# Six casts of value-weight sums behind the first tile's exponentials, and four raw row stores issued by SyncE

## The chip, the cores and the metric

The kernel runs on one core of one Trainium2 chip. The metric is the device time of one execution, in microseconds (us); smaller is better. Before the change it is 1594.4 us, the median of three runs (1594.2 to 1595.8).

## What is computed

A layer norm without weights feeds two branches, and their results are joined on the input. Sequence length S = 2048, width D = 576, 32 heads of 18 columns, hidden width F = 4608, all in float32.

```python
xn = _layernorm(x)
# branch A: linear attention with learned features
q, k, v = split_heads(xn @ wqkv)                  # 32 heads of 18
pq, pk = q @ w_phi, k @ w_phi                     # one 18x18 matrix per head
phi_q = concat(softmax(pq), softmax(-pq))
phi_k = concat(softmax(pk), softmax(-pk))
kv = sum over s of phi_k[s] (outer) v[s];  z = sum over s of phi_k[s]
s  = (phi_q @ kv / (phi_q @ z + 1e-6)) @ wo
# branch B: gated feed-forward
g  = silu((silu(xn @ w_gate) * (xn @ w_up)) @ w_down)
out = x + s * g
```

## The kernel before

Every float32 operand of a matmul is split into a rounded high part (a cast on ScalarE, ACT in the profile) and a low part (the operand minus the high part, on VectorE = DVE or GpSimd = POOL), and a product takes three matmuls: high by high, high by low, low by high. TensorE is PE in the profile, SyncE is SP. Names such as TH and TL are the high and the low part of one matrix.

The work has four stages. The **first** (0 to 61 us of the trace) reads x in four blocks of 512 rows, normalizes them, turns them with PE, splits them into `XB`, folds `w_phi` into the q and k weights, and computes the first tiles of the feed-forward as filler for PE. The order of all this is written out by hand: the wrappers `PE`, `ACT`, `DVE`, `POOL` and `SP` of class `InOrder` keep each engine's instructions in the order of the program text. Blocks are taken in the order b = 2, 3, 0, 1. For each block `x_raw(b)` (line 271) copies 64 turned columns from PSUM to a tile `xr` on ScalarE and stores it into `x_dram` with two DMAs, which ScalarE issues. `xr` has one buffer; GpSimd reads it too (`x_rest_low`, line 266) for blocks 3, 0 and 1.

The **second** stage (61 to about 221 us) computes k, its features, v, and the sum kv over 16 row tiles of 128. `k_tile` (line 653) makes the product for k in PSUM (`p`), then `softmax_parts` (line 525): DVE takes maxima and minima per head and subtracts them (lines 530 and 531), ScalarE takes the exponentials (line 534, two per tile, collected in `exps`), DVE sums (538), takes reciprocals (661) and scales (662) to `phi`. `v_plain` (line 671) makes half of v in one of the PSUM banks vx, vy, vw, and `v_copy` (646) copies it on ScalarE into `vbuf`. `kv_step` (line 543) adds phi times v to `kvp` on PE, one tile later than phi was begun.

From the fifth tile on, v is computed with Strassen's scheme, which needs sums and differences of blocks of x ("stacked sums", `raw_x`, `sums`, `sum_parts`, lines 560 to 582) and of the value weights (`v_sums(c)`, line 589, for the three row chunks c = 0, 1, 2). `v_sums(c)` loads two rows of weights with SyncE (line 599), makes four sums on GpSimd (600 to 603), and then twice casts a sum on ScalarE into TH (606) and takes the low part on GpSimd (608 for c < 2, 610 for c = 2). The buffers of c = 0 (`sraw`) are used again by c = 2 and afterwards by the stacked sums; those of c = 1 by other loads (line 121 among them). All three calls stand in the program after the first tile's `k_tile` and `v_plain`, and before the second tile's. `v_first` (612) needs PE to be done with a part of the value weights.

The **third** stage (to 491 us) makes q, the attention output and more feed-forward tiles, the **fourth** the rest of the feed-forward.

Outside the first stage the compiler's scheduler orders each engine's queue: it takes instructions by priority (earlier in the program first, `tc.high_priority()` ahead) as they become ready in its own estimate of time. An engine executes its queue strictly in that order. `tc.issue_after(ins)` adds an edge: the block's instructions on the engine of `ins` are queued behind `ins`. It adds no semaphore.

Of the kernel before, what the change touches and what calls it, by code (L numbers as in the profile page):

```python
# [61 lines left out]
def gated_hedgehog_kernel(ctx: ExitStack, tc, x, w_qk, w_v, consts_in, wo, w_gu, w_tail, w_down, out):  # L62
# [5 lines left out]
    nc = tc.nc  # L68
# [19 lines left out]
    x_dram = dram.tile([2, 4, P, 4, P], F32, name="x_dram")  # L88
# [67 lines left out]
    with ExitStack() as att:  # L156
# [18 lines left out]
        with ExitStack() as wst:  # L175
# [4 lines left out]
            with ExitStack() as pst:  # L180
# [12 lines left out]
                PE, ACT, DVE, POOL, SP = (InOrder(tc, e) for e in (nc.tensor, nc.scalar, nc.vector, nc.gpsimd, nc.sync))  # L193
# [77 lines left out]
                def x_raw(b, ps):  # L271
                    xr = prep.tile([P, 2, BT], F32, name="xr", bufs=1)
                    ACT.copy(xr, ps)
                    for m in range(2):
                        ACT.dma_start(x_dram[b // 2, :, :, b % 2 * 2 + m].rearrange("s p n -> p s n"),
                                      xr[:, m].rearrange("p (s n) -> p s n", s=4))
                    return xr

                def fold(m, g, ps=None):
# [90 lines left out]
                t = slice(8, 12)  # L370
# [22 lines left out]
                ACT.copy(first_weights[0][1][0], raws[1])  # L393
                part_low(first_weights[0][1], raws[1])
                x_raw(2, ps)
                load_x(1)
                half(0, 0)
# [10 lines left out]
                for n in range(6):  # L408
                    o = n * D if n < 3 else 832 + (n - 3) * D
                    wv[n] = ahead[1 if n < 3 else 3][:, o:o + D]  # L410
                    k, c = V_PLACES[n]
                    SP.dma_start(wv[n], w_v[:, k, c])
                stat(12, 13, 14, 15)
                t = slice(12, 16)
# [25 lines left out]
                for c in range(2):  # L440
                    x_high(3, c, tops[c])
                    x_low(3, c, tops[c])
                x_rest_high(3, tops[2])
                xr = x_raw(3, tops[2])
                x_rest_low(3, POOL, xr)
                stat(2, 3)
# [8 lines left out]
                t = slice(0, 8)  # L455
# [26 lines left out]
                for c in range(2):  # L482
                    x_high(0, c, tops[c])
                    x_low(0, c, tops[c])
                x_rest_high(0, tops[2])
                xr = x_raw(0, tops[2])
                x_rest_low(0, POOL, xr)
                products(1, 1, 1, "h0 h1")
# [18 lines left out]
                xr = x_raw(1, tops[2])  # L507
# [8 lines left out]
            TH = kt.tile([P, 3, 3, HALF], F32R, name="TH")  # L516
# [24 lines left out]
            kk_pool, read, exps = kk, [], []  # L541
# [47 lines left out]
            def v_sums(c):  # L589
                if c == 1:  # L590
                    u = epool.tile([P, 2, 3, P], F32, name="raw", bufs=2).rearrange("p a b n -> p (a b n)")[:, 0:D]
                    l = kk.tile([P, 4, 2, P], F32, name="slo", bufs=1).rearrange("p a b n -> p (a b n)")[:, 0:D]
                else:
                    t = kk.tile([P, 4, 3, P], F32, name="sraw", bufs=1).rearrange("p a b n -> p (a b n)")
                    u, l = t[:, 0:D], t[:, D:2 * D]
                u, l = (t.rearrange("p (m n) -> p m n", m=2) for t in (u, l))
                add, sub = nc.gpsimd.tensor_add, nc.gpsimd.tensor_sub
                for k, t in enumerate((u, l)):
                    nc.sync.dma_start(t, w_v[:, k, c].rearrange("p (m n) -> p m n", m=2))
                sub(l[:, 0], l[:, 0], u[:, 0])  # L600
                sub(t1[:, c] if c < 2 else t1t, u[:, 0], u[:, 1])
                add(u[:, 1], u[:, 1], l[:, 0])
                sub(l[:, 1], l[:, 1], u[:, 1])
                for m, t in ((0, u[:, 1:2]), (slice(1, 3), l)):
                    m = slice(0, 1) if m == 0 else m
                    nc.scalar.copy(TH[:, m, c], t)
                    if c < 2:
                        nc.gpsimd.tensor_sub(TL[:, m, c], t, TH[:, m, c])
                    else:
                        nc.gpsimd.tensor_sub(TH[64:96, m, 2], t[64:96], TH[64:96, m, 2])  # L610
# [71 lines left out]
            for p in range(8):  # L682
                k = (p + 4) % 8
                ts = [k // 4 * HT + k % 4 + 4 * j for j in range(2)]
                if p < 2:
                    for j, t in enumerate(ts):
                        phi = k_tile(t)
                        v_plain(t, vbuf[j], 0)
                        if pend is not None:
                            if not kvp:  # L690
                                kvp += [kps.tile([GW, 4, GW + 1], F32, name=f"kvp{i}") for i in range(3)]
                            kv_step(*pend)
                        v_plain(t, vbuf[j], 1)
                        pend = (2 * p + j, phi, vbuf[j])
                        if p == 0 and j == 0:
                            for c in range(3):
                                v_sums(c)
                        elif p == 0:
                            load_stack(order[0])
                            raw_x(order[0], 0, 1)  # L700
                            raw_x(order[0], 2, 3)
                        elif j == 0:
                            sums(order[0])
                    if p == 1:
                        v_first()
                        sum_parts(order[0])
                        load_stack(order[1])
                    continue
# [750 lines left out]
```

## Time and profile before

| what | value |
|---|---|
| median of the runs | 1594.4 us (1594.2, 1594.4, 1595.8) |
| the profiled execution's own time | 1593.34 us |
| its span (first to last instruction) | 1591.5 us |
| mean granted clock of PE | 0.998 |
| DVE, ACT, POOL busy | 73%, 46%, 42% |

How to read what follows. A timeline row has the start (us from the span's start), the length, the engine, the line, the operation, output and inputs with shapes, a count, and in brackets the idle time of the engine before it with what ended that. Neighbouring instructions of one kind are merged into one row with a count, and its length then runs from the first start to the last end. Instructions of the first stage that are kept in order by hand all have line 50, the wrapper's. An engine name with a q (SPq, ACTq) is its sequencer, here issuing DMAs. PE and PEld are one engine's matmuls and weight loads. A row of the chain has start, length, engine, tile, line and count.

### The profile page before, as it was taken

How to read it: one execution, taken by the hardware profiler on the slowest of the kernel's cores; microseconds unless marked ns; L12 is line 12 of the kernel's file. 1: busy time of each engine (PE TensorE's matmuls, PEld its weight loads, DVE VectorE, ACT ScalarE, POOL GpSimd, SP SyncE). 2: the span in 40 equal slices, each digit the busy share in tenths (PEclk: the TensorE clock that was granted, in tenths of full speed). 3: DMA queues.
4: the chain of work that ended last, by engine and by line, in shares of the span. 5: the costliest groups of instructions: out<-in, count | busy, mean ns of one | idle time of the engine just before them, and what ended most of it. 6: DMA issues, size and time to landing. Idle time of an engine off the chain costs nothing.

```text
span 1591.5 us, 25302 instructions
## 1 busy us (share of the span) xinstructions
PE 1574.4 (99%) x9371; PEld 1417.9 (89%) x9371; DVE 1166.4 (73%) x1720; ACT 729.3 (46%) x1406; POOL 672.4 (42%) x725
## 2 busy tenths in 40 slices
PE   9899999999999999999999999999999999999998
PEld 7799998999988898898888898888888888888887
DVE  7577769999957778887777778645667667666677
ACT  6633345454535645454444544454343343333334
POOL 5755672444116635644545445223324324133133
PEclk9999999999999999999999999999999999999999
DMA  9414344446448554555555453975545565556445
GB/s 288 144 57 146 113 135 137 123 124 195 138 148 270 178 177 171 180 172 179 175 177 202 159 192 116 338 218 151 154 139 154 183 188 160 175 184 185 142 118 179
DMA packets 123303, 269.05 MB, mean 169 GB/s; under 512 B 12452, under 2 KB 54116, under 8 KB 121900
## 3 DMA queue, kind: packets, MB, share of 16 engines
q1 hardware_dynamic: 108620, 245.67, 47.1%
q0 software_dynamic: 3552, 12.59, 2.8%
q10 hardware_dynamic: 11008, 9.18, 1.8%
q8 instruction: 74, 1.21, 0.3%
q14 instruction: 49, 0.40, 0.1%
HBM read 167.54 MB, written 99.09 MB: 168 GB/s over the span
## 4 chain that ended last, share of the span: by engine, by line
PE 92%; DVE 2%; POOL 2%; ACT 1%; issue 1%; DMA 1%; SPq 0%; ACTq 0%; POOLq 0%
PE px L1006 25%; PE pd L1127 24%; PE pw L1006 12%; PE p L108 7%; PE py L1006 6%; PE pe L108 5%; PE p L888 4%; PE kvp L547 2%; PE pt L860 2%; PE vx L635 1%; PE pt L853 1%; PE vw L635 1%; PE vx L108 0%; PE vy L108 0%; DMA wst<-in_A_w_qk 0%
## 5 line engine op out<-in xcount | busy, mean ns | idle before, releaser
L1127 PEld LDWEIGHTS pd<-dw,hh 128*128 128x128 f32 x3012 | 423.4, 188 | 22.7 <-ACT pd L1182 1.5
L1127 PE MATMUL pd<-dw,hh 128*128 128x288 f32 x3012 | 437.7, 295 | 2.1 <-ACT pd L1182 0.7
L1006 PE MATMUL px<-X,w 128*128 128x512 f32 x1512 | 385.7, 390 | 0.0
L1006 PEld LDWEIGHTS px<-X,w 128*128 128x128 f32 x1512 | 274.6, 188 | 46.0
L1006 PE MATMUL pw<-X,w 128*128 128x512 f32 x744 | 188.8, 389 | 0.0
L1006 PEld LDWEIGHTS pw<-X,w 128*128 128x128 f32 x744 | 139.6, 188 | 28.9
L1289 DVE TENSOR_TENSOR acc<-pd,acc 128x576 f32<-128x576 f32 x128 | 96.3, 753 | 92.6 <-PE pd L1127 92.1
L1040 DVE TENSOR_TENSOR s<-pw,s 128x512 f32<-128x512 f32 x126 | 86.4, 687 | 89.6 <-ACT s L1035 79.2
L1035 ACT COPY s<-px 128x512 f32<-128x512 f32 x126 | 73.8, 586 | 145.4 <-PE px L1006 145.2
L73 ACT CAST hh<-ha 128x512 fp32r<-128x512 f32 x140 | 82.7, 619 | 94.2 <-PE pd L1127 68.7
L74 DVE TENSOR_TENSOR hh<-ha,hh 128x512 fp32r<-128x512 f32 x140 | 110.4, 814 | 19.4 <-ACT hh L73 19.1
L1261 POOL TENSOR_TENSOR hb<-hb 128x512 f32<-128x512 f32 x34 | 46.7, 1375 | 157.1 <-DVE hb L1052 156.8
L74 DVE TENSOR_TENSOR w<-ld,w 128x512 fp32r<-128x512 f32 (+1 forms) x96 | 78.1, 815 | 40.4 <-ACT w L73 39.6
L1006 PE MATMUL px<-X,wt 128*128 128x512 f32 x252 | 98.0, 389 | 0.0
L1006 PE MATMUL py<-X,w 128*128 128x512 f32 x378 | 96.5, 390 | 0.0
L1274 POOL TENSOR_TENSOR ha<-ha 128x512 f32<-128x512 f32 x34 | 52.6, 1564 | 100.9 <-DVE hh L74 100.9
L1248 POOL TENSOR_TENSOR h<-ha,hb 128x512 f32<-128x512 f32 x34 | 44.7, 1313 | 105.6 <-DVE ha L1056 76.1
L982 POOL TENSOR_TENSOR ts<-ld 128x256 f32<-128x256 f32 x32 | 27.0, 842 | 138.7 <-issue 67.5
L73 ACT CAST w<-ld 128x512 fp32r<-128x512 f32 (+1 forms) x96 | 52.7, 550 | 71.6 <-POOL ld L985 41.8
L1060 ACT COPY py<-px 128x512 f32<-128x512 f32 x63 | 36.1, 572 | 106.6 <-PE px L1006 95.0
L108 PE MATMUL pe<-X,wh 128*128 128x512 f32 x260 | 80.4, 395 | 0.0
L1006 PEld LDWEIGHTS py<-X,w 128*128 128x128 f32 x378 | 68.3, 188 | 10.8
(317 smaller groups left out, 3246.9 us busy)
## 6 DMA issues: line engine op xcount, KB each, us to landing
w_dram<-w SPq DMA_DIRECT2D x90, 512.0 KB
w<-w_dram SPq DMA_DIRECT2D x90, 512.0 KB
wt<-t_dram SPq DMA_DIRECT2D x62, 336.0 KB
ld<-in_B_w_gu SPq DMA_DIRECT2D x32, 512.0 KB
rt<-in_B_w_down SPq DMA_DIRECT2D x33, 288.0 KB
rb<-in_B_w_down SPq DMA_DIRECT2D x33, 288.0 KB
w_dram<-w SPq DMA_DIRECT2D x30, 256.0 KB
w<-w_dram SPq DMA_DIRECT2D x30, 256.0 KB
```

The lines of the kernel that those rows point to most:

```text
L73: nc.scalar.copy(hi, src)
L74: nc.vector.tensor_sub(lo, src, hi)
L108: last = nc.tensor.matmul(ps, l, r, start=n == 0, stop=n == len(pairs) - 1)
L888: nc.tensor.matmul(ps[:, 0:HALF], a, bw, start=k == 0, stop=k == len(mm) - 1)
L1006: nc.tensor.matmul(ps, l, r, start=first and n == 0, stop=last and n == len(mm) - 1, skip_group_check=True)
L1035: snaps.append(nc.scalar.copy(t, ps))
L1040: nc.vector.tensor_add(t, ps, t)
L1127: nc.tensor.matmul(ps, l, r, start=first and n == 0 and m == 0, stop=n == len(hs) - 1 and m == 2, skip_group_check=True)
L1248: sub(s, g["h"][0][0], g["h"][0][1])
L1261: nc.gpsimd.tensor_add(a21, a21, g["h"][1][1])
L1274: sub(a12, a12, g["h"][0][0])
L1289: nc.vector.tensor_add(a2, pd[:, :, 0:HALF], a2)
```

## The change

Two edits. In `x_raw` the two stores of blocks 0 and 3 are issued by SyncE (also in program order, by its wrapper) instead of ScalarE; blocks 1 and 2 stay as they are. In `v_sums` both casts of line 606 are put into `tc.issue_after(exps[-1].ins)`, for each c; when `v_sums` is called, `exps` ends with the first tile's second exponential. The low parts on GpSimd, which read the casts, and the loads get no edge of their own.

```diff
                     for m in range(2):
-                        ACT.dma_start(x_dram[b // 2, :, :, b % 2 * 2 + m].rearrange("s p n -> p s n"),
-                                      xr[:, m].rearrange("p (s n) -> p s n", s=4))
+                        (SP if b in (0, 3) else ACT).dma_start(x_dram[b // 2, :, :, b % 2 * 2 + m].rearrange("s p n -> p s n"),
+                            xr[:, m].rearrange("p (s n) -> p s n", s=4))
                     return xr
...
                     m = slice(0, 1) if m == 0 else m
-                    nc.scalar.copy(TH[:, m, c], t)
+                    with tc.issue_after(exps[-1].ins):
+                        nc.scalar.copy(TH[:, m, c], t)
                     if c < 2:
                         nc.gpsimd.tensor_sub(TL[:, m, c], t, TH[:, m, c])
```

## The prediction

> **What bounds the kernel now.** I read the page first, then the windows, then PE's, ACT's, DVE's, POOL's and SP's timelines around the two edits, and the chain behind them.
>
> ```profile
> span 1591.5 us, 25302 instructions
> ...
> PE 1574.4 (99%) x9371; PEld 1417.9 (89%) x9371; DVE 1166.4 (73%) x1720; ACT 729.3 (46%) x1406; POOL 672.4 (42%) x725
> ```
>
> TensorE is busy 99% of the span, so an edit on another engine is worth only the idle time or the slow time of PE that it removes. The windows (length, then busy time and count of each engine, granted clock, DMA share, GB/s) show where there is any near the edits:
>
> ```profile
> 30.00:56.00 26.00, 25.75 (x180) 23.13 (x179) 23.68 (x52) 20.95 (x31) 18.21 (x28) 1.00 0.69 224
> 56.00:61.10 5.10, 4.90 (x34) 4.06 (x32) 4.09 (x10) 4.26 (x6) 0.71 (x1) 1.00 0.69 232
> 74.40:81.40 7.00, 0.02 (x1) 0.05 (x1) 3.43 (x4) 5.73 (x12) 6.31 (x8) 0.80 0.19 56
> 81.40:83.40 2.00, 2.00 (x9) 2.00 (x10) 1.93 (x4) 0.67 (x2) 1.92 (x3) 0.50 0.03 8
> ```
>
> From 74.4 to 81.4 us PE does nothing, and right after it the clock is granted at a half. PE's timeline names the wait:
>
> ```profile
> 81.38 4.20 PE L547 MATMUL kvp<-v,phi 128*126 128x127 f32 x20 [7.02 <-DVE phi L662]
> ```
>
> The first `kv_step` waits 7.02 us for the first tile's phi, written by VectorE at line 662. VectorE in turn:
>
> ```profile
> 67.38 0.76 DVE L531 TENSOR_TENSOR phi<-p,m 128x576 f32<-128x576 f32 x1
> 77.90 1.35 DVE L538 TENSOR_REDUCE sm<-phi 128x64 f32<-128x1152 f32 x1 [9.76 <-ACT phi L534]
> 79.28 0.55 DVE L661 RECIPROCAL sm<-sm 128x64 f32<-128x64 f32 x1
> 79.87 1.36 DVE L662 TENSOR_TENSOR phi<-phi,sm 128x1152 f32<-128x1152 f32 x1
> ```
>
> It has the exponentials' arguments ready at 67.38 + 0.76 = 68.14 and then sits 9.76 us for ScalarE's exponentials. ScalarE's timeline says why:
>
> ```profile
> 73.75 0.43 ACT L606 CAST TH<-raw 128x288 fp32r<-128x288 f32 x1 [3.97 <-POOL raw L602]
> 74.62 0.67 ACT L606 CAST TH<-slo 128x576 fp32r<-128x576 f32 x1 [0.45 <-POOL slo L603]
> 75.31 1.28 ACT L534 ACT_TABLE_LOAD   x1
> 76.61 1.26 ACT L534 ACTIVATE phi<-phi 128x576 f32<-128x576 f32 x2
> 78.45 0.83 ACT L77 CAST wh<-raw 128x768 fp32r<-128x768 f32 x1 [0.59 <-DMA raw<-in_B_w_gu]
> 79.19 0.45 ACT L646 COPY v<-vx 128x252 f32<-128x252 f32 x2
> 79.53 0.53 ACT L646 COPY v<-vy 128x90 f32<-128x90 f32 x3
> 79.92 1.05 ACT L606 CAST TH<-sraw 128x288 fp32r<-128x288 f32 x2
> ```
>
> The exponentials stand behind the casts of line 606 for c = 0 and 1, and those wait for GpSimd's sums (3.97 and 0.45 us). ScalarE idles there while the exponentials' arguments lie ready. This is a wrong order in one queue, not a lack of engine time.
>
> **The casts (line 606).** With the edit the first tile's two exponentials stand ahead of all six casts. The table load in front of them, 1.28 us, either runs early in idle time or waits for an argument. At worst it starts at 68.14, when the last argument is ready: the exponentials run 69.4 to 70.7, and DVE's three steps (77.90 to 81.23, 3.33 us) end at 74.0. At best only the second exponential, 0.63 (half of 1.26), follows 68.14: it ends at 68.8, phi at 72.1. The chain of waits gives PE's order after that:
>
> ```profile
> 81.38 4.20 PE kvp L547 x20
> 85.58 1.92 PE vx L108 x14
> 87.49 3.71 PE p L108 x28
> 91.20 1.85 PE vy L108 x14
> 93.05 2.06 PE kvp L547 x20
> ```
>
> PE is free for `kv_step` at 81.38 - 7.02 = 74.36. Phi is there between 72.1 and 74.0, so the whole 7.02 us goes. The next thing that could be late is the first tile's v: five copies, 79.19 to 80.06, 0.87 us, of banks that PE filled long before. ScalarE does them behind the exponentials at 69 to 71.5, or even behind the casts of c = 1. GpSimd's rows bound that:
>
> ```profile
> 65.73 0.80 POOL L601 TENSOR_TENSOR raw<-sraw 128x288 f32<-128x288 f32 x1
> ...
> 68.26 0.81 POOL L603 TENSOR_TENSOR sraw<-sraw 128x288 f32<-128x288 f32 x1
> 69.02 2.27 POOL L608 TENSOR_TENSOR TL<-sraw,TH 128x288 fp32r<-128x288 f32 x2
> ...
> 102.67 0.79 POOL L617 TENSOR_TENSOR KVWH<-h,KVWH 32x288 fp32r<-32x288 f32 x1 [10.81 <-ACT KVWH L615]
> ```
>
> Four sums take 65.73 to 69.07, 3.34 us, so all eight of c = 0 and 1 are done at 72.4, the last cast (0.67) at 73.1 and the copies at 74.0. Still in time.
>
> **The slow clock.** The first `kv_step` takes 4.20 us where the next, the same 20 instructions, takes 2.06; the vx group behind it takes 1.92 where vy, of the same 14, takes 1.85. The granted clock was 0.50 in 81.4 to 83.4. The stall thus costs a second time: 2.14 + 0.07 = 2.21 us. With no stall this goes as well, and 2.21 us, measured on this very stall, is the term of the sum. The Trainium skill ("TensorE: Matmul & The Clock Gate", Part 1: The HAM clock gate) says that the array drops to half rate after an idle window of about 3.4 us and needs about 3.4 us of work to return. By that rule the slow time would cost an estimated 1.7 us and the sum would be 0.5 us smaller. The trace agrees that the clock halves after a wait of 7.02 us, and shows a slow time somewhat longer than the page's.
>
> **What the casts' delay costs.** The casts are done about as early as GpSimd's sums allow, but TL of c = 0 now comes behind the eight sums: 72.4 + 2.27 = 74.7 instead of 71.3, and the load for c = 2 waits for it in SyncE's queue. Behind that load stand line 121's and line 558's:
>
> ```profile
> 40.29 1.59 SPq L50 DMA_DIRECT2D wst<-in_A_w_qk  x2
> 55.80 0.83 SPq L599 DMA_DIRECT2D sraw<-in_A_w_v  x2
> ...
> 71.32 0.80 SPq L599 DMA_DIRECT2D sraw<-in_A_w_v  x2
> 75.37 0.33 SPq L121 DMA_DIRECT2D raw<-in_B_w_gu  x1
> ```
>
> So c = 2 runs up to 3.4 us later on GpSimd. What hides this is the wait of 10.81 us ahead of line 617, which depends on PE. PE now arrives there 9.2 us earlier, so the cover shrinks to 1.6 us, and 3.4 us of delay would leave line 617 at most 1.8 us late. On PE the first product with the stacked sums waits for it:
>
> ```profile
> 110.96 0.30 PE L635 MATMUL vw<-KVWH,shi 128*128 128x288 f32 x1
> ```
>
> That is 8.3 us after line 617, more than the few operations of GpSimd between them should take. I cost the delay at nothing; without that cover it would be the 1.8 us.
>
> **The stores.** Four of the eight stores of `x_raw` leave ScalarE's queue (b = 3, the first row, and b = 0, the second):
>
> ```profile
> 34.58 2.52 ACTq L50 DMA_DIRECT2D x_dram<-xr  x2
> ...
> 49.62 1.10 ACTq L50 DMA_DIRECT2D x_dram<-xr  x2
> 50.76 0.79 ACT L50 CAST QH<-tp 128x756 fp32r<-128x756 f32 x1 [1.17 <-PE tp L50]
> ```
>
> Of b = 0: the cast of QH can start up to 1.17 us sooner, if PE's product is ready then; the row names PE as the last releaser, so it may also be nothing. PE has 0.25 us of idle time in 30 to 56 and 0.20 in 56 to 61.1, and its own work fills the rest, so both blocks of stores together can shorten PE by 0.45 us unless its busy spans hide waits. I take 0.45, between 0 and 1.1; b = 3 adds nothing to it, since those 0.25 us are all that PE waits in 26. On SyncE the stores of b = 3 come before the loads at 40.29 and those of b = 0 before the loads at 55.80. Their source is ready at 34.58 and 49.62, when ScalarE issued them, so they hold up little behind them: 2.52 us at most for b = 3, ahead of loads that are next needed by the products for q some 10 us later. In DMA, b = 3 now shares SyncE's queue in a stretch (30 to 56) where DMA is 0.69 busy; the bytes are the same, and the buffer is next written only shortly before 49.62. I cost it at zero, and at 2.5 us if those loads came too late.
>
> **The sum.** 7.02 + 2.21 + 0.45 = 9.68 us. The profiled execution took 1593.34 us (span 1591.5 and 1.84 around it), so it would take 1583.66. The median of the runs, 1594.4, lies 1.06 above it: 1584.7. PE is idle for 1591.5 - 1574.4 = 17.1 us in all, and 7.0 of them are this stall; the other 10 lie in 1500 us, so little is there to swallow the gain and it should reach the end.
>
> **The rivals.**
>
> *A new wait at the second tile* (0.15). The compiler sets each queue's order by its own estimate of readiness; it could put the casts of c = 2 before the second tile's exponentials. In the trace they run at 79.92, and that tile's exponentials later. The load goes out at 74.7, and a load of this kind takes from 3.1 us (75.37 to 78.45 for line 121) to 6.1 us (71.32 until three sums, 2.5 us, before the cast at 79.92); then four sums, 3.34 us; the cast, 0.67; exponentials, 1.26; DVE, 3.33: phi at 86.4 to 89.4. PE wants it at 74.36 + 2.06 + 1.85 + 3.71 + 1.85 = 83.8. That is a stall of 2.6 to 5.6 us, at the upper end perhaps with 2.2 us of slow clock: a gain of 7.1 down to 1.9 us, 1587.3 to 1592.5. Against it: c = 2 now starts later also in the compiler's estimate, while the second tile's arguments come sooner.
>
> *The order does not change where it matters* (0.07). If the first tile's v copies land behind the cast of line 77 and its load, `kv_step` waits as before: line 121's load goes out after TL of c = 1, at 74.7 + 2.27 = 77.0, lands at 80.1, the cast ends at 80.9 and the copies at 81.8, where phi ended the wait at 81.23 before. Stall and slow clock stay, 0.6 us longer, less 0.45: 1594.5. For it: that cast stands before the copies now. Against it: its load depends on the casts that the edit moves back.
>
> *Slower* (0.04). The same copies behind the casts of c = 2: load at 74.7, landed at 80.8 by the 6.1 us above, sums 84.1, both casts 85.2, line 77's 0.83, copies 0.87: 86.9 against 81.38. PE would lose 5.5 us more, less 0.45: 1599.4. It decides once the compiler holds c = 2's sums for ready before the first v; in the trace the copies stand before them (79.19 against 79.92).
>
> **How the numbers follow.** The full gain has 0.74 and gives 1582.8 to 1587, from a store term of 0 to 1.1, 1.8 us of late GpSimd, and runs that lie 1 us apart. The 2.5 us of late loads would still give 1587.2. With the nearer half of the first rival the range is 1582.5 to 1589.5. A difference of 0.2%, 3.2 us, is about what can be told from none. Faster takes the full gain and nearly all of the first rival, 0.88; same takes the second rival and the rest, 0.08; slower 0.04.
>
> **What would show it.** In the new profile the wait of `kvp` L547 for phi L662 is gone, PE runs through 74 us at a clock of 1.00, the first `kv_step` takes 2.06 us, and the two exponentials stand before the first cast of line 606 on ScalarE, at 67 to 69. PE's idle time in 30 to 61 falls by up to 0.45. I am wrong if a wait of PE for phi or v remains anywhere before 110 us, or if the products with the stacked sums (line 635) wait for GpSimd.

## The result and the profile after

The changed kernel takes 1583.74 us, the median of 6 runs (1582.93 to 1586.63), beside 1594.95 us (1594.2 to 1595.8, also 6 runs) of the kernel before. The ratio is 0.9932 with a 95% interval of 0.9919 to 0.9945, which is 8.8 to 12.9 us less. The profiled execution of the changed kernel took 1583.69 us. In the code after, every line from 606 on has a number higher by one.

The page of the profile after has the same work on every engine in a shorter span:

```profile
span 1581.9 us, 25306 instructions
...
PE 1570.4 (99%) x9371; PEld 1415.3 (89%) x9371; DVE 1163.2 (74%) x1720; ACT 728.9 (46%) x1406; POOL 671.5 (42%) x725
```

PE has the same 9371 matmuls. Its busy time is 4.0 us less, which is slow or hidden waiting time and not work, and its idle time falls from 17.1 to 11.5 us. The windows of the kernel after, with the columns as before:

```profile
30.00:56.00 26.00, 25.92 (x186) 23.53 (x184) 23.70 (x54) 21.63 (x32) 18.88 (x28) 1.00 0.73 223
56.00:61.10 5.10, 5.10 (x35) 4.45 (x34) 2.58 (x7) 3.53 (x5) 1.44 (x2) 1.00 0.71 253
74.40:81.40 7.00, 7.00 (x57) 7.00 (x56) 3.95 (x4) 1.86 (x5) 5.89 (x7) 1.00 0.43 140
81.40:83.40 2.00, 1.80 (x16) 1.57 (x15) 1.93 (x4) 1.71 (x6) 1.92 (x3) 1.00 0.00 0
```

From 74.4 to 81.4 us PE was idle for 6.98 us before; now it is busy throughout, at a clock of 1.00. In 81.4 to 83.4 something new shows: 0.20 us of idle time.

To see where the time went, the span is cut at points that both traces have. On PE's timeline of the kernel before these are the second fold (the group of 24), the first product for k, the second tile's product for k, and the second `kv_step`; the first `kv_step`, at 81.38, was shown above:

```profile
20.57 2.84 PE L50 MATMUL tp<-PHI,wst 126*128 126x126 f32 x24
...
61.12 0.40 PE L108 MATMUL p<-KVWH,X 128*128 128x288 f32 x1
...
87.33 0.29 PE L108 MATMUL p<-KVWH,X 128*128 128x288 f32 x1
...
92.89 2.23 PE L547 MATMUL kvp<-v,phi 128*126 128x127 f32 x20
```

The same points, and the first `kv_step`, after:

```profile
20.12 2.84 PE L50 MATMUL tp<-PHI,wst 126*128 126x126 f32 x24
...
59.63 0.40 PE L108 MATMUL p<-KVWH,X 128*128 128x288 f32 x1
...
72.87 2.18 PE L547 MATMUL kvp<-v,phi 128*126 128x127 f32 x20
...
76.80 0.29 PE L108 MATMUL p<-KVWH,X 128*128 128x288 f32 x1
...
82.72 2.33 PE L547 MATMUL kvp<-v,phi 128*126 128x127 f32 x20 [0.20 <-ACT v L647]
```

| stretch | before | after | difference |
|---|---|---|---|
| start to second fold | 20.57 | 20.12 | -0.45 |
| second fold to first product for k | 40.55 | 39.51 | -1.04 |
| to the first `kv_step` | 20.26 | 13.24 | -7.02 |
| to the second tile's product for k | 5.95 | 3.93 | -2.02 |
| to the second `kv_step` | 5.56 | 5.92 | +0.36 |
| to the end | 1498.6 | 1499.2 | +0.6 |

The sum is the spans' 9.6 us. The first row lies ahead of both edits: in the ten traces of this study the second fold starts between 19.54 and 22.60 us, whatever the kernel, so it is no effect of the change. The last row lies within the spread of the traces too (1498.5 to 1499.5 in the nine of them whose second `kv_step` ran at the full clock). What is left are four terms: the stall, the slow clock, about 1.0 us in the first stage, and a small loss at the second `kv_step`.

The median fell by 11.2 us, 1.6 us more than the traces differ. The traced execution of the kernel before (1593.34 us, mean clock 0.998) is a fast one of its kind. Of the 33 runs of that kernel beside the experiments one has 0.998 (1592.24 us); the 13 at 0.997 took 1594.2 us in the mean, the 17 at 0.996 1594.9, and the two below that 1597.0. So most executions of it probably have more slow clock than the trace; no second trace of it shows this.

ScalarE's timeline after shows the new order:

```profile
59.61 1.92 ACTq L50 DMA_DIRECT2D x_dram<-xr  x2
...
63.47 1.28 ACT L534 ACT_TABLE_LOAD   x1
65.67 0.69 ACT L534 ACTIVATE phi<-phi 128x576 f32<-128x576 f32 x1 [0.92 <-DVE phi L531]
67.12 0.69 ACT L534 ACTIVATE phi<-phi 128x576 f32<-128x576 f32 x1 [0.77 <-DVE phi L531]
67.72 0.44 ACT L647 COPY v<-vx 128x252 f32<-128x252 f32 x2
68.04 0.53 ACT L647 COPY v<-vy 128x90 f32<-128x90 f32 x3
68.43 1.05 ACT L607 CAST TH<-sraw 128x288 fp32r<-128x288 f32 x2
72.02 0.43 ACT L607 CAST TH<-raw 128x288 fp32r<-128x288 f32 x1 [2.54 <-POOL raw L602]
72.91 0.67 ACT L607 CAST TH<-slo 128x576 fp32r<-128x576 f32 x1 [0.45 <-POOL slo L603]
73.49 0.68 ACT L534 ACTIVATE phi<-phi 128x576 f32<-128x576 f32 x1
...
80.20 0.83 ACT L77 CAST wh<-raw 128x768 fp32r<-128x768 f32 x1 [5.11 <-DMA raw<-in_B_w_gu]
80.94 0.43 ACT L607 CAST TH<-sraw 128x288 fp32r<-128x288 f32 x1
81.69 0.68 ACT L607 CAST TH<-sraw 128x576 fp32r<-128x576 f32 x1 [0.32 <-POOL sraw L603]
82.27 0.51 ACT L647 COPY v<-vx 128x90 f32<-128x90 f32 x3
```

The first tile's exponentials run at 65.67 and 67.12, as soon as DVE has their arguments; the waits for GpSimd's sums (2.54 and 0.45 us) now lie behind them. They still delay the second tile's exponentials (73.49, where VectorE has the argument at 72.79), but PE does not wait for that tile's phi. The last row is the new wait: three copies of the second tile's v stand behind a cast that waits 5.11 us for its load and behind the casts of c = 2, and the second `kv_step` waits 0.20 us for them.

The first tile's phi is finished by DVE, and the delayed sums meet line 618 (617 before) on GpSimd, as two rows show:

```profile
69.82 1.50 DVE L663 TENSOR_TENSOR phi<-phi,sm 128x1152 f32<-128x1152 f32 x1
```

```profile
92.61 0.79 POOL L618 TENSOR_TENSOR KVWH<-h,KVWH 32x288 fp32r<-32x288 f32 x1 [0.44 <-ACT KVWH L616]
```

Phi is ready at 71.32, 1.55 us before PE wants it. At line 618 GpSimd still waits, though only 0.44 us of the 10.81 us are left.

### The profile page after: what moved, and what is told of

Same layout as the page of the kernel before. It is cut to its first block, busy times and chain, and to the rows that moved or that the text cites. A ratio compares the mean times of both kernels' runs of the same rounds, so it can differ in the third digit from the quotient of the medians.

```text
span 1581.9 us, 25306 instructions
## 1 busy us (share of the span) xinstructions
PE 1570.4 (99%) x9371; PEld 1415.3 (89%) x9371; DVE 1163.2 (74%) x1720; ACT 728.9 (46%) x1406; POOL 671.5 (42%) x725
## 4 chain that ended last, share of the span: by engine, by line
PE 95%; POOL 1%; DVE 1%; DMA 1%; issue 1%; ACT 0%; SPq 0%; POOLq 0%; ACTq 0%
PE px L1007 25%; PE pd L1128 24%; PE pw L1007 12%; PE p L108 7%; PE py L1007 6%; PE pe L108 5%; PE p L889 4%; PE kvp L547 2%; PE pt L861 2%; PE pe L50 1%; PE vx L636 1%; PE pt L854 1%; PE tp L50 1%; PE vw L636 1%; DMA wst<-in_A_w_qk 0%
```

## The experiments

The forecast's account is that the order of ScalarE's queue gives nearly all of the gain, by the stall and by the slow clock that follows from it, and the stores a few tenths. The rivals to it: the stores carry a good part; the first `kv_step` is slow for another reason than the clock; order alone can bring a wait back at the second tile; and stores on SyncE hold up the loads behind them. The first four kernels ran beside one set of runs of the kernel before and the other four beside a second; the kernel before took 1594.72 us (24 runs) in the one and 1594.54 us (9 runs) in the other. Traces are compared from the second fold on, so that the start does not blur them.

**The casts alone.** The kernel before with

```diff
-                    nc.scalar.copy(TH[:, m, c], t)
+                    with tc.issue_after(exps[-1].ins):
+                        nc.scalar.copy(TH[:, m, c], t)
```

> Only the casts of line 606 behind the first tile's exponentials; all stores stay on ScalarE. Theory A (the stall of 7.0 us and 2.0 us of slow clock go, a new wait of about 0.5 us at the second kv_step comes): 8.5 us less than before, p still starts at about 61.1, first kv_step at 74.4 without a wait and about 2.0 us long. Rival B (the stores also matter for the stall, since they let the exponentials' arguments come sooner): under 7 us less, with some wait for phi left.

It took 1584.56 us (1584.14 to 1585.41), a ratio of 0.9933 [0.9921, 0.9945]. On PE's timeline:

```profile
74.69 2.18 PE L547 MATMUL kvp<-v,phi 128*126 128x127 f32 x20
...
84.57 2.33 PE L547 MATMUL kvp<-v,phi 128*126 128x127 f32 x20 [0.23 <-ACT v L647]
```

Stall and slow clock are gone, and the small wait at the second `kv_step` is there. The casts alone give the gain, as far as the medians can tell; what the stores add to it is inside the runs' spread. In the traces, from the second fold to the end, the casts alone give 7.9 us and both edits 9.2.

**The stores alone.** The kernel before with

```diff
-                        ACT.dma_start(...)
+                        (SP if b in (0, 3) else ACT).dma_start(...)
```

> Only the stores of blocks 3 and 0 issued by SyncE; the casts stay ahead of the exponentials. Theory A (ScalarE gets about 1.1 us back ahead of the cast of QH and PE passes it on): 1.0 us less than before, k's first product about 1.0 us earlier than the same point after the first fold, and the stall of 7.0 us and the half clock still there, shifted. Forecast's own value: 0.45 less. Rival B (the 1.5 us by which that product came earlier was the start of the run alone): nothing.

It took 1593.4 us (1592.34 to 1593.93), a ratio of 0.999 [0.9981, 0.9998]. PE's first product for k comes 39.53 us after the second fold, 1.02 us earlier than before. None of it is left in the trace at the second `kv_step`, which comes 72.66 us after the fold, and 72.32 before. PE's timeline and the window behind the stall (the columns as above):

```profile
80.80 4.23 PE L547 MATMUL kvp<-v,phi 128*126 128x127 f32 x20 [7.75 <-DVE phi L662]
```

```profile
80.80:86.20 5.40, 5.40 (x26) 5.40 (x27) 4.55 (x6) 1.72 (x4) 4.90 (x7) 0.50 0.17 52
```

PE arrives 1.02 us earlier at a stall that ends only 0.28 us earlier (60.53 us after the fold against 60.81), so the wait grows from 7.02 to 7.75 us. The slow clock after it lasts 5.40 us: the second tile's product for k, at 87.37, comes 6.57 us after the first `kv_step`, against 5.95 before. So -1.02 + 0.73 + 0.62 = +0.33 us. The stall thus takes most of what the stores gave, and leaves 0.3 us. The 0.62 us come from a slow clock that lasted longer than in the trace of the kernel before (the last section has the lengths), and need not be an effect of the edit. The runs point the other way: the median is 1.3 us lower, and at equal mean clock the five runs at 0.996 and the five at 0.997 are 1.3 and 0.9 us below the 13 and nine of the kernel before. The trace does not show from where, and this stays open.

**Filling the stall.** The kernel before, with 36 matmuls of no use put on PE ahead of the first `kv_step`, into a bank that is not in use yet.

```diff
+                                for _ in range(36):
+                                    nc.tensor.matmul(kvp[2][:, 0:3, 0:GW], idle[:, 0:GW], idle[:, 0:GW].unsqueeze(1).to_broadcast([P, 3, GW]),
+                                                     start=True, stop=True, skip_group_check=True)
```

> The kernel before, with 36 idle bf16 products of 126x378 put on PE between the second tile's vw product and the first kv_step, into a bank that kv_step starts afresh; they take about 6 of the 7 us of the stall. Theory A (the slow first kv_step is the clock's answer to the idle time): still a wait for phi, of about 1 us, but kv_step takes 2.0 instead of 4.0 and the total is 2.0 us less than before. Rival B (it is slow for its operands, fresh from DVE and ACT): kv_step stays at 4 us and the time is as before.

```profile
73.17 5.95 PE L693 MATMUL kvp<-idle 128*126 128x378 bf16 x36
81.06 2.25 PE L547 MATMUL kvp<-v,phi 128*126 128x127 f32 x20 [1.93 <-DVE phi L662]
```

It took 1592.44 us (1591.29 to 1594.11), a ratio of 0.9985 [0.9976, 0.9994], 1.0 to 3.8 us less. Phi is no earlier than before (the wait ends 61.52 us after the second fold, against 60.81), but after a wait of only 1.93 us the same 20 matmuls take 2.25 us and not 4.20. The slow time is a consequence of PE's idleness and not of late operands, and on its own it is worth about 2 us: the second tile's product for k follows the first `kv_step` by 4.00 us and not by 5.95.

**The edge for c = 1 only.** The changed kernel with

```diff
-                    with tc.issue_after(exps[-1].ins):
+                    with tc.issue_after(exps[-1].ins) if c == 1 else ExitStack():
```

> The changed kernel, but only the casts for c = 1 are tied to the exponentials; those of c = 0 are queued ahead of the exponentials, and those of c = 2 and the cast of line 77 then stand ahead of the second tile's exponentials. Theory A (what counts is which cast that waits long stands ahead of which exponentials): no wait of the first kv_step for phi beyond 0.5 us, but a new stall of about 2.5 us at the second one, total about 2 us above the changed kernel. Rival B (any cast ahead of the first exponentials brings the stall back): 5 to 9 us above the changed kernel.

It took 1591.01 us (1589.68 to 1594.79), a ratio of 0.9978 [0.9967, 0.9988]: 7.3 us of the gain are lost. PE's timeline, the window from the second `kv_step` on, and ScalarE's timeline:

```profile
74.13 2.25 PE L547 MATMUL kvp<-v,phi 128*126 128x127 f32 x20 [1.59 <-DVE phi L663]
...
87.26 4.32 PE L547 MATMUL kvp<-v,phi 128*126 128x127 f32 x20 [3.40 <-DVE phi L663]
```

```profile
87.26:92.60 5.34, 5.34 (x26) 5.34 (x27) 4.49 (x6) 1.71 (x4) 2.70 (x3) 0.50 0.00 0
```

```profile
66.40 0.43 ACT L607 CAST TH<-sraw 128x288 fp32r<-128x288 f32 x1 [4.27 <-POOL sraw L602]
...
69.27 1.26 ACT L534 ACTIVATE phi<-phi 128x576 f32<-128x576 f32 x2
...
76.30 0.43 ACT L607 CAST TH<-sraw 128x288 fp32r<-128x288 f32 x1 [2.82 <-POOL sraw L602]
77.18 0.68 ACT L607 CAST TH<-sraw 128x576 fp32r<-128x576 f32 x1 [0.45 <-POOL sraw L603]
81.10 0.83 ACT L77 CAST wh<-raw 128x768 fp32r<-128x768 f32 x1 [3.25 <-DMA raw<-in_B_w_gu]
81.84 0.68 ACT L534 ACTIVATE phi<-phi 128x576 f32<-128x576 f32 x1
```

c = 0's casts now stand ahead of the first tile's exponentials again and wait 4.27 us for GpSimd's sums, so the exponentials run at 69.27. And c = 2's casts, and line 77's cast with its load, land ahead of the second tile's exponentials (81.84, where the changed kernel has 73.49). This is the forecast's first rival, a stall at the second tile. PE waits 1.59 us at the first `kv_step` and 3.40 at the second, and the second wait brings the slow clock back: the third tile's product for k comes 6.70 us after the second `kv_step` instead of 4.03. That is 1.59 + 3.28 + 2.67 = 7.5 us, less 0.6 in the rest of the trace. The expectation was wrong in size, and about the first `kv_step`, whose wait was to be at most 0.5 us. The loss of 7.3 us falls into the range of its rival B, a return of the first stall, but only 1.59 us of it lie there; the rest is the second tile's stall, as theory A has it. It is larger because the load's wait of 3.25 us also stands before these exponentials, and because the stall is long enough for the clock.

**The second tile's copies first.** The changed kernel with `v_sums(2)` called later and its casts behind the copies of v:

```diff
-                    with tc.issue_after(exps[-1].ins):
+                    with tc.issue_after((copied if c == 2 else exps)[-1].ins):
...
+            copied = []
...
-                    nc.scalar.copy(d, src)
+                    copied.append(nc.scalar.copy(d, src))
...
-                            for c in range(3):
+                            for c in range(2):
...
+                            v_sums(2)
```

> The changed kernel, with the casts of c = 2 also queued behind the second tile's last copies of v. Theory A (the 0.2 to 0.5 us wait left at the second kv_step comes from copies of v standing behind those casts): that wait goes, 0.4 to 0.5 us less than the changed kernel in the trace, in the median hardly visible. Rival B (the wait is for the cast of line 77 and its load, which still stand ahead of the copies): the wait stays.

```profile
84.11 2.23 PE L547 MATMUL kvp<-v,phi 128*126 128x127 f32 x20
```

```profile
81.68 0.51 ACT L649 COPY v<-vx 128x90 f32<-128x90 f32 x3
82.43 0.43 ACT L607 CAST TH<-sraw 128x288 fp32r<-128x288 f32 x1 [0.23 <-POOL sraw L602]
```

The copies (line 649 in this kernel) now stand before c = 2's casts, the second `kv_step` has no wait, and it comes 9.49 us after the first instead of 9.85. From the fold to the end the trace is 0.4 us shorter than that of the changed kernel. The median, 1583.85 us (1582.81 to 1585.23), cannot show this. By the trace it is the best order here; it is not shown to be faster.

**Which stores.** The changed kernel with `b in (0,)`, with `b in (3,)` and with `b in (0, 1, 2, 3)`.

> The changed kernel, but only block 0's stores are issued by SyncE. Theory A (block 0 brings all of the stores' gain, block 3 none): as the changed kernel within 0.3 us. Rival B (block 3's 2.5 us on ScalarE count too): 0.5 to 1 us more.

> The changed kernel, but only block 3's stores are issued by SyncE. Theory A (block 0 brings all of it): 1.0 us more than the changed kernel. Rival B (block 3 counts): between 0 and 0.5 us more.

> The changed kernel with all eight stores of x_raw issued by SyncE. Theory A (after block 1's stores ScalarE only has to be in time for the exponentials, which have slack; block 2's stand ahead of the silu of the first feed-forward tile, but PE is busy there): as the changed kernel within 0.3 us. Rival B (block 2's 1.0 us on ScalarE is passed on as block 0's was): 0.5 to 1 us less. Rival C (block 2's stores hold up SyncE's loads of x behind them): 0.5 to 1 us more.

They took 1584.57 (1583.21 to 1586.04), 1583.74 (1583.57 to 1584.25) and 1583.70 us (1583.51 to 1584.91), ratios of 0.9938 [0.9925, 0.995], 0.9934 [0.9921, 0.9946] and 0.9933 [0.992, 0.9947]. The medians do not tell these apart. The traces do, in the stretch from the second fold to the first product for k:

| stores on SyncE | us | kernels |
|---|---|---|
| none | 40.55, 40.67, 40.55 | before, the casts alone, the filled stall |
| b = 3 | 40.38 | `b in (3,)` |
| b = 0 | 39.52 | `b in (0,)` |
| b = 0 and 3 | 39.51, 39.53, 39.51, 39.52 | after, the stores alone, the edge for c = 1, the copies first |
| all four | 39.51 | `b in (0, 1, 2, 3)` |

The two ends of that stretch for `b in (3,)`, on PE's timeline:

```profile
20.20 2.84 PE L50 MATMUL tp<-PHI,wst 126*128 126x126 f32 x24
...
60.58 0.40 PE L108 MATMUL p<-KVWH,X 128*128 128x288 f32 x1
```

In this stretch block 0's stores are worth 1.03 us and give all of it; block 3's give at most 0.2 alone and nothing beside block 0's. That it reaches the end is not shown: the trace with `b in (3,)`, 0.87 us behind the changed kernel here, takes as long from the second fold to the end (within 0.1 us), and its median is the same, where the expectation had 1.0 us more. The median with `b in (0,)` is 0.8 us higher, where at most 0.3 was expected, and its trace from the fold to the end is as long too. What follows the second `kv_step` differs by up to 1.0 us among the traces, which hides such a step. Moving block 1's stores as well puts the loads of line 599 behind them in SyncE's queue. GpSimd's and PE's timelines of `b in (0, 1, 2, 3)`:

```profile
65.52 0.80 POOL L601 TENSOR_TENSOR raw<-sraw 128x288 f32<-128x288 f32 x1 [2.10 <-DMA sraw<-in_A_w_v]
```

```profile
83.56 2.33 PE L547 MATMUL kvp<-v,phi 128*126 128x127 f32 x20 [0.95 <-ACT v L647]
```

GpSimd waits 2.10 us for its first sum's operand. In the changed kernel it waits 2.41 us for VectorE at nearly the same place, so from the second fold the first sum comes only 0.07 us later (45.18 against 45.11) and the third 0.34. The wait at the second `kv_step` grows from 0.20 to 0.95 us, and that step comes 0.62 us later. At most this is what moving two more blocks costs: not all of it is traced to the loads, and the median, 1583.70 us, shows none of it. So the split of the stores in the change, two blocks moved and two left, does not show a gain by block 3, and in these traces block 1 is better left where it is.

## Why the prediction was right

**The stall.** As forecast, all 7.02 us went. PE was free 1.49 us earlier than the forecast had it (72.87 against 74.36, 0.45 by the earlier start and 1.04 by the first stage), phi was ready at 71.32, and the first tile's v was copied at 67.7 to 68.6, ahead of the casts. Of the two cases that the forecast left open for the table load the better one came: it ran at 63.47, before DVE had written the exponentials' argument, so that neither it nor the casts stood in the way.

**The slow clock.** Right in mechanism, as the filled stall shows, and 2.02 us instead of 2.21. The forecast compared the row of 4.20 us with one of 2.06 from the chain; the distance between PE's rows, from the `kv_step` to the next tile's product (5.95 and 3.93 us), is the better measure, because it holds no overlap. How long the slow clock lasts differs between executions, so 2.02 us is the cost in this trace; in two others it was 2.6 and 2.7 us.

**The stores.** Here a term of the sum was mis-sized: 0.45 us forecast from the idle time of PE, 1.03 us measured in the first stage, which is still inside the bounds of 0 to 1.1. The forecast took PE's idle time for all that it can win, unless its busy spans hide waits. They do. The last 60 fold products, before:

```profile
48.26 4.28 PE L50 MATMUL tp<-PHI,wst 126*128 126x126 f32 x36
...
52.80 2.98 PE L50 MATMUL tp<-PHI,wst 126*128 126x126 f32 x24 [0.25 <-issue]
```

and after, in one row:

```profile
47.74 6.83 PE L50 MATMUL tp<-PHI,wst 126*128 126x126 f32 x60
```

The same 60 matmuls lasted from 48.26 to 55.78, 7.52 us, and last 6.83 now: 0.69 us less, of which the view called only 0.25 idle. From the start of these rows to the start of the next product (55.73 before, 54.40 after) it is 0.81 us, which leaves 0.56 hidden in rows that look busy: the row's length runs to the end of its last matmul and does not show a late one inside. The upper bound, the cast's wait of 1.17 us on ScalarE, was the nearer row.

**The delayed sums.** Costed at nothing, rightly: line 618 still waits for what comes before it (0.44 us), so the delay stayed inside its cover, though that cover is nearly used up.

**What was not foreseen.** The forecast called itself wrong if a wait of PE for phi or v remained before 110 us, and one remains: the second tile's copies of v stand behind casts that wait, 0.20 us of wait, 0.36 us in the distances. The forecast looked for such a stand only for the first tile's copies (its second and third rivals) and for the second tile's exponentials (the first). The first rival did not come with the change, but it did with the edge for c = 1 only; there its price, 2.6 to 5.6 us of stall, held (3.40 us), with the slow clock on top.

With these sizes the forecast's sum would have been 7.02 + 2.02 + 1.03 - 0.36 = 9.71 us instead of 9.68. The total came out well partly by luck, because a term that was too small and a loss that was missing lay close together. The traces differ by 9.6 us, the medians by 11.2; the forecast of the median, 1584.7 us, lies 1.0 us above the measured 1583.74, which is inside its range.

## What to carry to other kernels

Where the engine that is nearly always busy waits, look at the queue of the engine that should have served it: an instruction that waits for something else, ahead of ones whose operands lie ready, can cost its whole wait, and putting it behind them makes that wait harmless without making anything faster. Order every instruction that waits in such a queue, and not only the one that is in the way now: with one edge instead of three 7 of the 11 us were lost again, most of them at the next tile. A gain ahead of a stall can be lost in it (0.3 of 1.02 us were left in the trace of the stores alone), and a busy span in a trace can hide a wait twice as long as the idle time beside it.

## What the runs showed of the hardware

**Where the clock falls.** After idle times of 1.59 and 1.93 us (the edge for c = 1, the filled stall) `kv_step` ran at 1.00 and took 2.25 us; after 3.40, 7.02 and 7.75 us it ran at 0.50 and took 4.20 to 4.32. The whole slow stretch, in windows of the kernel before, the stores alone and the edge for c = 1 (the columns as before), with a clock of 1.00 on both sides of each:

```profile
78.58:85.41 6.83, 4.03 (x21) 4.06 (x21) 5.94 (x8) 4.11 (x12) 6.17 (x8) 0.50 0.05 15
```

```profile
75.97:86.21 10.24, 5.41 (x26) 5.44 (x27) 7.97 (x9) 5.54 (x15) 9.17 (x12) 0.50 0.19 62
```

```profile
86.14:92.97 6.83, 5.71 (x27) 5.74 (x28) 5.94 (x8) 1.71 (x4) 3.82 (x3) 0.50 0.00 0
```

The clock fell 4.22, 2.92 and 2.28 us after PE's last matmul. From PE's restart the half rate lasted 4.03, 5.41 and 5.71 us, and cost 2.0, 2.6 and 2.7 us. The Trainium skill ("TensorE: Matmul & The Clock Gate", Part 1: The HAM clock gate) gives about 3.4 us for both, in a window that runs freely, so that the moment varies. The traces agree that it varies, and with the length of the window: the stretches differ by 10.24 - 6.83 = 3.41 us, and are two, three and two times as long as that. Each return came when the last 3.41 us of the stretch had been all work. The traces differ from the Trainium skill in the fall: 2.28 us without a matmul were enough once, less than a whole window.

**What two stores hold up.** The two store instructions of block 1, which no kernel but one moves, held ScalarE's sequencer for 1.92 us in the trace after and for 0.93 us before:

```profile
61.09 0.93 ACTq L50 DMA_DIRECT2D x_dram<-xr  x2
```

The same two instructions took 0.93 us also in the edge for c = 1, the copies first, `b in (0,)` and `b in (3,)`, and 1.67 to 2.13 us with the casts alone, the stores alone and the filled stall. Neither edit goes with the longer time, and with one trace of each kernel it is not shown what does.

**The table load runs ahead.** In the trace after it starts at 63.47, 2.2 us before the activation it serves, which waits for its argument meanwhile. So it can fill an idle time.
